# Attention, a gated MLP and a phase mixer in one launch: the pool of xT opened first, float64 by bit masks in wide pieces, 1/(2π) put into w_theta, and a new table for the order

## The chip, the cores and the metric

The kernel runs on one core of a Trainium2 chip. The metric is the device time of one execution in microseconds; executions of the kernel before took 879.43 us in the median of three, from 874.92 to 885.33 us. PE is TensorE, DVE is VectorE, ACT is ScalarE, POOL is GpSimd, and SP is SyncE, which here only issues transfers.

## The reference, cut to what matters

Batch 4, 8 heads, 576 positions, 64 columns a head, so 512 columns a position. The weights w_in, w_out, w_theta, w_tok and w_ch are float64 in memory, the rest is float32.

```python
scores = scale * q @ k.T + bias            # bias: a small network of log positions, one per head
x = softmax(scores) @ v                    # heads side by side: (4, 576, 512)

h = gelu_tanh(x @ w_in)                    # 512 -> 1024
u, v = h[..., :512], h[..., 512:]
v = w_sg @ layernorm(v) + b_sg             # 576 x 576 over the positions
x = x + (u * v) @ w_out

theta = x @ w_theta
y = w_tok_r @ (x * cos(theta)) + w_tok_i @ (x * sin(theta))
u = x + y
out = u + relu(u @ w_ch)
```

## The kernel before

**Tiles.** Heads go in pairs, so attention is 16 pairs (four batches by four), named by batch and pair: `xT0_2` belongs to batch 0, pair 2. A pair has nine score tiles of 128 rows by 576 columns: four for each head and one (kind 2) that holds the last 64 rows of both. A tile runs through every engine: scores `s` (PE, PSUM); `e`, the scores plus bias with their maximum (DVE, a custom operation); the exponential (ACT); `p`, a float16 upper part (ACT) and its residual (POOL, sometimes DVE); the transposed `pT` (a DMA transpose that SP issues); and `px`, the product with v (PE, one PSUM tile, 14 matmuls a score tile). After a pair's nine tiles the product is scaled into `xf` (four tiles) and `xfr` (the kind-2 tile), flipped by PE against the identity into `xq`, copied as two float16 parts into `xT` and also stored to memory. `xf` and `xfr` have one buffer each, `e` has four, `pT` eight.

**The MLP of a batch** reads `xT` and the converted `w_in` (`wi`): `vp`, gelu, the norm `n`, then `up` and `sp` (with w_sg), the product `gg` and its store. `s2` multiplies with w_out (`op`); `theta` makes `tp`, reduces it by multiples of 2π (`rk`, `rr`), takes sine and cosine and writes the products `z` in two parts; `ymix` (`yp`) mixes the positions, `s4` (`cp`) ends.

**PSUM.** The flips `xq`, the MLP's `vp`, `up` and `sp`, and the norms of the weights (`ps_wi`, `ps_ws`) share one ring of three buffers, handed out in the order in which the code asks for them (`cps`). A write to the ring therefore waits for the readers of the third request before it.

**SBUF.** Pools lie as a stack on each side. `xT` lives in pool `xTp`, opened after `w1_load` in `build`, so that it lies where the staging pool of `w1_load` (`wstage`, raw pieces of w_in and w_sg) was. A first write to it waits until that pool's work is done.

**Float64.** `conv64` turns a piece of raw pairs of words into float32. A weight's block of 128 rows goes in two halves of 256 (for w_tok 288) columns: three ACT operations (absolute value, sign, absolute value), two TENSOR_SCALAR and one SCALAR_TENSOR_TENSOR on DVE, and a product with the sign on POOL or DVE.

**The order.** The program is not run as written. A recorder (`Rec`) collects every operation with a key (its due time), an engine or a choice of engines, and what it depends on. `plan` lists the operations of each engine in the order of key plus `SHIFT[name]`, for a choice with `BIAS[name, engine]`, and emits them. All instructions are emitted by one helper line (379 before, 383 after), so the rows of the trace go by tile names. SP executes its list in order: loads and transposes stand in one queue, and an instruction whose buffer is not free holds those behind it.

**The stages of the profiled execution** (us from the start of the span): 0 to 108 the table of position biases (`hq` on DVE and ACT, `pb` on PE, `bs` on DVE or ACT); 108 to 238 pairs 0_1 to 0_3 with the conversion of w_in and w_sg; 238 to 441 batches 1 and 2 with the MLPs of 0 and 1; 441 to 539 batch 3 with MLP 2, and its drain; 539 to 690 MLP 3, `s2`, the conversion of w_out, w_theta, w_tok and w_ch, and the first `theta`; 690 to 880 the rest of `theta`, `ymix` and `s4`.

## Time and profile before

| | |
|---|---|
| median of three executions | 879.43 us (874.92 to 885.33) |
| the profiled execution | 881.56 us |
| its span, first to last instruction | 879.8 us |
| busy: PE | 762.3 us (87%) |
| busy: PE's weight loads, beside its matmuls | 534.8 us (61%) |
| busy: DVE | 629.9 us (72%) |
| busy: ACT | 520.5 us (59%) |
| busy: POOL | 298.4 us (34%) |
| moved by DMA | 115.52 MB, mean 131 GB/s |

The span is the time between the first and the last instruction of the profiled execution; about 1.8 us of its time lie around it. A busy share is a mean over stages with different limits, so the page's slices of 22 us and the sums by stage are read beside it.

### The profile page before, as it was taken

How to read it: one execution, taken by the hardware profiler on the slowest of the kernel's cores; microseconds unless marked ns; L12 is line 12 of the kernel's file. 1: busy time of each engine (PE TensorE's matmuls, PEld its weight loads, DVE VectorE, ACT ScalarE, POOL GpSimd, SP SyncE). 2: the span in 40 equal slices, each digit the busy share in tenths (PEclk: the TensorE clock that was granted, in tenths of full speed). 3: DMA queues.
4: the chain of work that ended last, by engine and by line, in shares of the span. 5: the costliest groups of instructions: out<-in, count | busy, mean ns of one | idle time of the engine just before them, and what ended most of it. 6: DMA issues, size and time to landing. Idle time of an engine off the chain costs nothing.

```text
span 879.8 us, 17586 instructions
## 1 busy us (share of the span) xinstructions
PE 762.3 (87%) x6544; PEld 534.8 (61%) x6544; DVE 629.9 (72%) x1475; ACT 520.5 (59%) x1038; POOL 298.4 (34%) x263
## 2 busy tenths in 40 slices
PE   5689778648899889997999976998878999999998
PEld 2234344326454555545654453687757999899998
DVE  5777558869698568986589754997989892763712
ACT  5777567865689447892579713655568671542500
POOL 0011244643567335672547531365433200000000
PEclk9979956557999999999799996999999999999999
DMA  7987689729898299866998396465622210010101
GB/s 227 217 169 172 169 184 192 150 87 192 158 186 154 72 221 179 169 150 133 190 188 151 77 179 159 133 198 173 180 82 64 74 54 1 1 55 1 41 14 54
DMA packets 205734, 115.52 MB, mean 131 GB/s; under 512 B 176593, under 2 KB 176849, under 8 KB 205649
## 3 DMA queue, kind: packets, MB, share of 16 engines
q1 hardware_dynamic: 198192, 101.01, 52.6%
q10 hardware_dynamic: 7456, 13.40, 5.0%
q8 instruction: 51, 0.84, 0.4%
q14 instruction: 35, 0.28, 0.1%
HBM read 47.13 MB, written 14.16 MB: 70 GB/s over the span
## 4 chain that ended last, share of the span: by engine, by line
PE 52%; DVE 17%; DMA 15%; issue 7%; ACT 5%; POOL 3%; SPq 1%; ACTq 0%; DVEq 0%; POOLq 0%
PE yp L379 12%; PE s L379 8%; PE cp L379 6%; DMA pT<-p 6%; PE pb L379 6%; PE sp L379 5%; PE tp L379 4%; PE up L379 4%; PE px L379 4%; PE vp L379 3%; POOL p L379 2%; DVE v L379 2%; DMA vr<-v_all 2%; DVE e L379 2%; DVE cvaw_tok L379 2%
## 5 line engine op out<-in xcount | busy, mean ns | idle before, releaser
L379 POOL TENSOR_TENSOR p<-e,p 128x576 f16<-128x576 f32 x144 | 191.0, 1338 | 183.3 <-ACT p L379 172.5
L379 PE MATMUL s<-kq 64*128 64x288 f32 (+1 forms) x640 | 149.1, 495 | 21.5 <-DVE m L379 21.5
L379 ACT ACTIVATE e<-e,m 128x576 f32<-128x576 f32 x144 | 110.6, 769 | 55.9 <-DVE m L379 44.7
L379 PEld LDWEIGHTS <-pT 128*128 128x128 f16 (+1 forms) x2240 | 86.0, 108 | 69.4 <-issue 30.4
L379 PE MATMUL px<-v,pT 128*128 128x64 f16 (+1 forms) x2240 | 95.4, 204 | 32.6 <-DMA pT<-p 21.9
L379 PE MATMUL yp<-wk,z 128*128 128x288 f32 x864 | 119.4, 297 | 1.5 <-ACT z L379 0.8
L379 DVE CUSTOM_DVE_ANT_0 e<-s,bias 128x576 f32<-128x576 f32 x128 | 94.6, 752 | 35.5 <-PE s L379 18.7
L379 PEld LDWEIGHTS yp<-wk,z 128*128 128x128 f32 x864 | 116.5, 190 | 2.6 <-ACT z L379 1.1
L379 PEld LDWEIGHTS s<-kq 64*128 64x128 f32 (+1 forms) x640 | 71.9, 199 | 65.8 <-DVE m L379 40.3
L379 ACT ACTIVATE p<-e 128x576 f16<-128x576 f32 x144 | 94.0, 674 | 29.7 <-DMA pT<-p 22.2
L379 PE MATMUL pb<-hq,w2s 128*32 128x288 f32 x576 | 69.3, 454 | 14.3 <-DVE bs L379 9.9
L379 PE MATMUL op<-sp_g,wo 128*128 128x288 f32 x384 | 60.8, 311 | 7.6 <-DVE x L379 4.1
L379 PE MATMUL vp<-wi,xT 128*128 128x512 f16 (+1 forms) x240 | 63.4, 397 | 1.4 <-DVE xT L379 1.4
L379 PEld LDWEIGHTS op<-sp_g,wo 128*128 128x128 f32 x384 | 54.4, 194 | 12.4 <-DVE x L379 4.9
L379 PEld LDWEIGHTS pb<-hq,w2s 128*32 128x32 f32 x576 | 28.4, 117 | 52.9 <-DVE bs L379 9.9
L379 PE MATMUL sp<-ws,n 128*128 128x64 f16 (+1 forms) x384 | 57.4, 287 | 0.3 <-DVE n L379 0.2
L379 PE MATMUL up<-xT,wi 128*128 128x64 f16 (+1 forms) x384 | 55.1, 287 | 0.7 <-DVE gtu L379 0.7
L379 ACT ACTIVATE sp_u<-x 128x576 fp32r<-128x576 f32 x16 | 10.8, 684 | 70.8 <-DVE x L379 70.1
L379 PE MATMUL cp<-sp_u,wc 128*128 128x288 f32 x384 | 52.5, 295 | 0.0
L379 PE MATMUL tp<-wt,sp_t 128*128 128x512 f32 x192 | 47.9, 403 | 4.3 <-DVE sp_t L379 2.6
L379 DVE TENSOR_SCALAR hq<-lt,sl,nb 128x576 f32<-128x576 f32 x96 | 49.8, 586 | 2.4 <-PE pb L379 1.6
L379 PEld LDWEIGHTS cp<-sp_u,wc 128*128 128x128 f32 x384 | 51.2, 188 | 0.2
(197 smaller groups left out, 1214.9 us busy)
## 6 DMA issues: line engine op xcount, KB each, us to landing
bias<-bs SPq DMA_DIRECT2D x32, 288.0 KB
kq<-kq SPq DMA_DIRECT2D x10, 576.0 KB
raww_tok<-w_tok SPq DMA_DIRECT2D x18, 288.0 KB
vr<-v_all SPq DMA_DIRECT2D x12, 384.0 KB
xx<-dx SPq DMA_DIRECT2D x16, 288.0 KB
out<-oo SPq DMA_DIRECT2D x16, 288.0 KB
dg<-gg SPq DMA_DIRECT2D x16, 256.0 KB
raw<-vp SPq DMA_DIRECT2D x12, 320.0 KB
```

What stands on the lines that cost most here:

```text
L379: getattr(getattr(self.nc, name), m)(*[res(x) for x in a], **out)
```

## The change

**Pools and buffers.** `xTp` is opened before `setup`, under all that is staged later, and is released last. `xf` has two buffers instead of one (`xfr` keeps one), `e` three instead of four, `pT` seven instead of eight. To make room, w_sg is loaded twice through one buffer (`ra`, then `rs`) instead of being kept, and v's sum of squares reads eight pieces of 1152 instead of twelve of 768.

**Float64.** With `fuse`, `conv64` takes a whole block (512 columns, for w_tok 576) at once: one ACT operation, two TENSOR_SCALAR and two SCALAR_TENSOR_TENSOR on DVE; the sign comes from a bit mask, and the product with it is gone. There are half as many loads, each twice as large. All five converted weights use it; the form with the sign stays in the code, unused.

**Theta.** w_theta is scaled by 1/(2π) when it is split, so that `tp` counts turns. A tile loses one TENSOR_SCALAR and one SCALAR_TENSOR_TENSOR of its DVE work; there are 18 tiles.

**Order.** The table is refitted, with an additional shift for each stage (`@a0` to `@a15` for the pairs, `@m`, `@o`, `@t`, `@y`, `@z` with the batch, `@w` and one for each weight). Against before, 36 residuals of `z` go from DVE to POOL, nine of the 36 `bs` additions go from DVE to ACT (18 and 18 before, 9 and 27 after), and the transfers of q and k go from ACT's queue to SP's (6 on ACT and 10 on SP before, 1 and 15 after). In bias_gen the matmuls of a group wait for all four `hq`.

```diff
-    def conv64(self, pool, dst, src, n, u):
+    def conv64(self, pool, dst, src, n, u, bufs, fuse=False):
...
-        nc.scalar.activation(a, hi.bitcast(F32), AF.Abs)
+        if fuse:
+            nc.scalar.activation(dst, hi.bitcast(F32), AF.Abs)
+            nc.vector.tensor_scalar(dst, dst, F64_MIN, F64_MAX, op0=ALU.max, op1=ALU.min)
+            nc.vector.tensor_scalar(di, di, 3, 0x3FFFFFF8, op0=ALU.logical_shift_left, op1=ALU.bitwise_and)
+            nc.vector.scalar_tensor_tensor(di, hi, TOP, di, op0=ALU.bitwise_and, op1=ALU.bitwise_or)
+            nc.vector.scalar_tensor_tensor(di, lo, 29, di, op0=ALU.logical_shift_right, op1=ALU.bitwise_or)
+            return
...
-        nc.vector.tensor_scalar(a, a, F64_MIN, F64_MAX, op0=ALU.max, op1=ALU.min)
-        nc.vector.tensor_scalar(ai, ai, 3, 0x40000000, op0=ALU.logical_shift_left, op1=ALU.bitwise_xor)
-        nc.vector.scalar_tensor_tensor(ai, lo, 29, ai, op0=ALU.logical_shift_right, op1=ALU.bitwise_or)
-        nc.scalar.activation(a, a, AF.Abs)
-        self.tt(("vector", "gpsimd"), dst, a, s, ALU.mult)
...
-        rs = sp.tile([P, 5, S], F32, name="rs")
...
+            rs = sp.tile([P, S], F32, tag="rs", bufs=1, name=f"ra{st}")
...
+            rs = sp.tile([P, S], F32, tag="rs", bufs=1, name=f"rs{st}")
...
-        s = a.tile([P, S], F32, tag="s", bufs=4, name=f"e{u}")
+        s = a.tile([P, S], F32, tag="s", bufs=3, name=f"e{u}")
...
-        pT = a.tile([P, 9, P], F16, tag="pT", bufs=8, name=f"pT{u}")
+        pT = a.tile([P, 9, P], F16, tag="pT", bufs=7, name=f"pT{u}")
...
-        xf = a.tile([P, 4, P], F32, tag="xf", bufs=1, name=f"xf{u}")
+        xf = a.tile([P, 4, P], F32, tag="xf", bufs=2, name=f"xf{u}")
...
-            nc.scalar.activation(k, ps, AF.Identity, scale=1.0 / (2 * math.pi), bias=self.magic)
-            nc.vector.tensor_scalar(k, k, MAGIC, None, op0=ALU.subtract)
-            nc.vector.scalar_tensor_tensor(r, k, -TWO_PI_HI, ps, op0=ALU.mult, op1=ALU.add)
-            nc.vector.scalar_tensor_tensor(r, k, -TWO_PI_LO, r, op0=ALU.mult, op1=ALU.add)
+            nc.scalar.activation(k, ps, AF.Identity, bias=self.magic)
+            nc.vector.scalar_tensor_tensor(r, k, MAGIC, ps, op0=ALU.subtract, op1=ALU.subtract)
...
+        self.p_x = nc.pool("xTp")
         self.setup()
...
         self.w1_load()
-        self.p_x = nc.pool("xTp")
...
-        for q in (self.ps_c, self.ps_x, self.p_c1, self.p_x, self.p_w1):
+        for q in (self.ps_c, self.ps_x, self.p_c1, self.p_w1, self.p_x):
```

Of the table, a line of each kind; the new `SHIFT` entries that begin with `@` are added to that of the name:

```diff
-    ("xT", "vector"): -9.533, ("xr", "scalar"): 42.3825, ("xr", "vector"): -78.4204,
+    ("xT", "vector"): -134.938, ("xr", "scalar"): -32.2441, ("xr", "vector"): 89.6171,
...
+    "@a0": -36.8725, "@a1": 84.4111, "@a10": -258.733, "@a11": -241.069, "@a12": 66.14, "@a13": 1.9727,
```

**Three places in the order.** First DVE where it first writes `xT`, in the second stage (108 to 238 us). `ih`, `gts`, `ghs` and `i2s` are small factors that follow the norm of one half of w_in, `v163` are pieces of v, `e0_3_1_3` is the score tile of pair 0_3, second head, last full tile. Before:

```order
L379 TENSOR_SCALAR gts0_132<-ih0_134 128x1
L379 TENSOR_SCALAR ghs0_133<-ih0_134 128x1
L379 CAST xT0_0_2097<-xq0_0_1802 128x512
L379 CAST xT0_0_2097<-xq0_0_2_2004 128x64
L379 TENSOR_TENSOR xT0_0_2097<-xq0_0_1802,xT0_0_2097 128x512
L379 ISA e0_3_1_3_2188,m0_3_1_3_1893<-s0_3_1_3_1925,bias3_75 128x576
```

Of the change:

```order
L383 TENSOR_TENSOR ih1_144<-fd_wi1_145,fd_v_152 128x1
L383 CAST xT0_0_170<-xq0_0_1509 128x512
L383 TENSOR_SCALAR i2s1_141<-ih1_144 128x1
L383 TENSOR_SCALAR ghs1_143<-ih1_144 128x1
L383 TENSOR_TENSOR xT0_0_170<-xq0_0_1509,xT0_0_170 128x512
L383 ISA e0_2_0_0_1494,m0_2_0_0_1429<-s0_2_0_0_1463,bias0_78 128x576
```

The first write of `xT0_0` has moved from the second half's factors (`ih0`) to the first half's (`ih1`), and from the eighth tile of pair 0_3 to the second tile of pair 0_2; the copy of the narrow flip `xq0_0_2`, which stood behind the first, is no longer beside it.

Second, DVE where the conversion of w_tok meets the first `theta`, at the end of the fifth stage (539 to 690 us). `tok4_0` is the first half of block 4, `wr_w_tok8` the whole block 8. Before:

```order
L379 TENSOR_SCALAR cvaw_tok4_0_8390<-cvaw_tok4_0_8390 128x288
L379 TENSOR_SCALAR rk0_4_8237<-rk0_4_8237 128x512
L379 TENSOR_SCALAR cvaw_tok4_0_8390<-cvaw_tok4_0_8390 128x288
L379 SCALAR_TENSOR_TENSOR rr0_4_8233<-rk0_4_8237,tp0_4_8145 128x512
L379 SCALAR_TENSOR_TENSOR cvaw_tok4_0_8390<-raww_tok4_0_8373,cvaw_tok4_0_8390 128x288
L379 SCALAR_TENSOR_TENSOR x1_3_8238<-xs3_0_8388,fd_v_153,op3_0_8336 128x576
L379 SCALAR_TENSOR_TENSOR rr0_4_8233<-rk0_4_8237,rr0_4_8233 128x512
L379 TENSOR_TENSOR wk_7223<-wr_w_tok3_8262,wk_7223 128x576
```

Of the change:

```order
L383 SCALAR_TENSOR_TENSOR wr_w_tok7_8031<-raww_tok7_8007,wr_w_tok7_8031 128x576
L383 SCALAR_TENSOR_TENSOR rr0_4_7982<-rk0_4_7986,tp0_4_7914 128x512
L383 SCALAR_TENSOR_TENSOR wr_w_tok7_8031<-raww_tok7_8007,wr_w_tok7_8031 128x576
L383 SCALAR_TENSOR_TENSOR x1_2_7096<-xs2_3_8081,fd_v_152,op2_3_8017 128x576
L383 TENSOR_TENSOR sp1_g3_8052<-gr3_1_7943,sp1_g3_8052 128x576
L383 TENSOR_TENSOR rw0_8045<-xp0_4_7912,rr0_4_7982 64x512
L383 TENSOR_SCALAR wr_w_tok8_8102<-wr_w_tok8_8102 128x576
L383 TENSOR_TENSOR wk_7097<-wr_w_tok7_8031,wk_7097 128x576
```

Theta's tile has one operation here where it had three, the conversion works on 576 columns, and it has come three to four blocks further by the same tile of theta.

Third, PE where MLP 2 ends and batch 3's attention drains, in the fourth stage (441 to 539 us). `sp2_3` and `sp2_4` are the last products of MLP 2, `s3_3_0_0` is the first score tile of the last pair's first head, and `xq3_0_2` the narrow flip of the batch's first pair. Before, where the last scores (of `s3_3_1_3`) stand 126 rows ahead of these:

```order
L379 LDWEIGHTS n16_2_5233
L379 MATMUL sp2_3_6694<-ws_1090,n16_2_5233 128x512
L379 LDWEIGHTS n16_2_5233
L379 MATMUL sp2_3_6694<-ws_1090,n16_2_5233 128x512
L379 MATMUL xq3_0_2_6697<-ident_160,xfr3_0_2_5526 128x64
```

Of the change:

```order
L383 MATMUL sp2_3_6457<-wsr_1078,nr_2_5064 128x512
L383 MATMUL s3_3_0_0_6482<-kq3_3_6127 128x288
L383 MATMUL s3_3_1_0_6504<-kq3_3_6127 128x288
L383 MATMUL s3_3_0_0_6482<-kq3_3_6127 128x288
L383 MATMUL s3_3_1_0_6504<-kq3_3_6127 128x288
L383 MATMUL xq3_0_2_6518<-ident_159,xfr3_0_2_5372 128x64
```

Scores of the last pair now stand between the last products of MLP 2; the last of them (`s3_3_1_3`) comes some 500 rows after these, among the products `px` of the last two pairs.

## Rows read from the trace of the kernel before

**Rows 1.** The page: busy tenths of PE, granted clock; 22 us a slice.

```profile
PE   5689778648899889997999976998878999999998
...
PEclk9979956557999999999799996999999999999999
```

**Rows 2.** Busy us by stage: stretch, length, each engine, clock, DMA share.

```profile
core 0: us, PE busy (x) PEld busy (x) DVE busy (x) ACT busy (x) POOL busy (x), PEclk, DMA share, GB/s
...
108.00:238.00 130.00, 91.91 (x774) 57.02 (x775) 97.38 (x293) 90.67 (x221) 62.30 (x56) 0.64 0.77 164
238.00:441.00 203.00, 186.60 (x1995) 109.31 (x1993) 153.37 (x416) 133.32 (x266) 111.84 (x93) 0.96 0.82 162
441.00:539.00 98.00, 81.04 (x917) 47.42 (x916) 69.18 (x186) 57.60 (x115) 47.98 (x41) 0.95 0.75 146
539.00:600.00 61.00, 60.54 (x369) 41.16 (x370) 52.46 (x110) 38.33 (x83) 25.00 (x23) 0.97 0.53 166
600.00:690.00 90.00, 74.95 (x497) 65.69 (x496) 83.20 (x149) 58.70 (x120) 35.98 (x31) 0.94 0.40 118
690.00:880.00 190.00, 185.58 (x1307) 178.88 (x1305) 101.53 (x164) 68.62 (x119) 5.27 (x6) 1.00 0.09 31
```

**Rows 3.** Tiles: ns min/median/max, first and last start; flip copies, norm.

```profile
L379 DVE CAST xT<-xq x32: 206/432/692, 205.4 to 538.4; 128x512 f16<-128x512 f32 x16, 128x64 f16<-128x64 f32 x16
...
L379 PE MATMUL ps_wi<-ssw,ones x4: 353/364/374, 164.1 to 196.0; 128*128 128x2 f32 x4
```

**Rows 4.** SP's queue, 167 to 215 us: start, us, issue, count.

```profile
167.51 1.32 SPq L379 DMA_TRANSPOSE pT<-p  x1
...
198.49 16.58 SPq L379 DMA_TRANSPOSE pT<-p  x8
```

**Rows 5.** Busy time in two short stretches, columns as in Rows 2.

```profile
160.00:200.00 40.00, 20.22 (x84) 11.89 (x85) 29.99 (x95) 30.61 (x81) 17.78 (x19) 0.50 0.44 106
520.00:536.00 16.00, 7.34 (x110) 4.94 (x109) 0.29 (x2) 0.68 (x1) 1.57 (x2) 0.80 0.97 162
```

**Rows 6.** DVE, ACT, POOL on cvawi, cvaw_tok, cvaw_theta, cvaw_ch, cvaw_out in turn.

```profile
0.00:880.00 880.00, 23.47 (x48) 12.93 (x32) 12.46 (x16) 0.92 0.58 131
...
0.00:880.00 880.00, 25.32 (x54) 15.69 (x36) 19.66 (x18) 0.92 0.58 131
...
0.00:880.00 880.00, 13.95 (x24) 6.78 (x16) 6.67 (x8) 0.92 0.58 131
...
0.00:880.00 880.00, 10.00 (x24) 6.50 (x16) 6.87 (x8) 0.92 0.58 131
...
0.00:880.00 880.00, 10.47 (x32) 6.64 (x16) 0.92 0.58 131
```

**Rows 7.** Tiles again: conversion of w_tok; theta's rk and rr.

```profile
L379 DVE TENSOR_SCALAR cvaw_tok<-cvaw_tok x36: 294/301/1348, 597.2 to 678.3; 128x288 f32<-128x288 f32 x18, 128x288 int32<-128x288 int32 x18
...
L379 DVE SCALAR_TENSOR_TENSOR cvaw_tok<-raww_tok,cvaw_tok x18: 444/448/946, 600.6 to 679.2; 128x288 int32<-128x288 int32 x18
...
L379 DVE TENSOR_SCALAR rk<-rk x18: 409/422/1516, 630.9 to 823.9; 128x512 f32<-128x512 f32 x18
...
L379 DVE SCALAR_TENSOR_TENSOR rr<-rk,rr x18: 677/684/1776, 634.8 to 826.4; 128x512 f32<-128x512 f32 x18
```

**Rows 8.** PE in time: a px group waits; then ACT's queue there.

```profile
532.50 0.93 PE L379 MATMUL px<-v,pT 128*128 128x64 f16 x14 [3.11 <-DMA pT<-p]
...
527.67 1.55 ACTq L379 DMA_DIRECT2D raww_out<-w_out  x2
```

**Rows 9.** A two-input operation on POOL, and z's residual on DVE.

```profile
L379 POOL TENSOR_TENSOR gg<-gg,gtu x20: 730/1277/1371, 283.4 to 611.6; 128x512 f32<-128x512 f32 x16, 128x256 f32<-128x256 f32 x4
...
L379 DVE TENSOR_TENSOR z<-rk,z x18: 677/684/1293, 645.6 to 832.2; 128x512 fp32r<-128x512 f32 x18
```

**Rows 10.** One score tile in time: e on DVE, its residual on POOL.

```profile
262.21 0.76 DVE L379 CUSTOM_DVE_ANT_0 e<-s,bias 128x576 f32<-128x576 f32 x1 [0.34 <-PE s L379]
...
266.68 2.52 POOL L379 TENSOR_TENSOR p<-e,p 128x576 f16<-128x576 f32 x2 [1.74 <-DVE mv L379]
```

More of the change, by code (lines that the diff above doesn't have):

```diff
@@ L253 @@
-    "xp": -331.5337, "xq": 298.6439, "xr": -67.349, "xs": -569.332, "xx": -233.673, "yp": -63.1746,
-    "z": 114.4221, "zb": 275.7247,
-}
-LOADF, LOADK = 1.8093412586188697, 8.575464505639914
-BV = 1.52008187476998
[5 rows of a table added]
+    "@w_ch": 85.8307, "@w_out": 57.1349, "@w_theta": 160.7065, "@w_tok": 95.8549, "@y0": -210.6919,
[3 rows of a table added]
+    "fa_ws": 1413.4328, "fb_v": 82.4448, "fb_wi": -819.9933, "fb_ws": -1094.933, "fc_v": 668.3878,
+    "fc_wi": -1320.5823, "fc_ws": 855.392, "fd_v": -186.6568, "fd_wi": -384.6853, "fd_ws": 954.7819,
@@ L729, in bias_gen @@
         self.ld(self.ident, d["ident"])
-        for i in range(12):
-            nc.key = 1.0 + 5 * i
-            vr = st.tile([P, 768], F32, tag="vr", bufs=2, name=f"vr{i}")
-            self.ld(vr, d["v_all"][:, i * 768:(i + 1) * 768], ("sync",))
+        for i in range(8):
+            nc.key = 1.0 + 7.5 * i
+            vr = st.tile([P, 1152], F32, tag="vr", bufs=2, name=f"vr{i}")
+            self.ld(vr, d["v_all"][:, i * 1152:(i + 1) * 1152], ("sync",))
             nc.scalar.activation(vr, vr, AF.Square, accum_out=self.ss_v[:, i:i + 1])
@@ L747, in w1_load @@
         self.eps4 = c.tile([P, 1], F32, name="eps4")
[L748 removed]
+        ssa = c.tile([P, 2, 4], F32, name="ssa")
         ssw = c.tile([P, 2, 2], F32, name="ssw")
@@ L1217, in build @@
         self.s2(0, t + 15, 3)
-        self.conv_w(self.wt, "w_theta", DM, 4, t + 15, 3)
+        self.conv_w(self.wt, "w_theta", DM, 4, t + 15, 3, 1.0 / TWO_PI)
         self.s2(1, t + 35, 3)
```

150 lines of the change are left out of this document (78 added, 72 removed), and 42 rows, old and new, of tables (BIAS, SHIFT).

## The prediction

> **What bounds the kernel now.** I read the page's slices first: PE is the busiest engine in most of them, and the granted clock stands near full except in slices 5 to 9 (counted from 0), 110 to 220 us, where it falls to 0.5 and PE's own digits are low [rows 1]. So I went by stage. The difference between a stage's length and PE's busy time is what the stage can give back without touching PE's work [rows 2]: 108 to 238 us, 130.0 − 91.9 = 38.1 us (at a clock of 0.64, so its matmuls run long as well); 238 to 441, 16.4; 441 to 539, 17.0; 539 to 690, 0.5 + 15.0 = 15.5; 690 to 880, 4.4. The last stage is PE's and gives nothing.
>
> Then the waits of each stage. In the second, the first copy of a flip into `xT` starts at 205.4 us and the last norm of w_in (`ps_wi`) is made at 196.0 [rows 3]; SP's queue issues no transpose between 167.5 + 1.3 and 198.5 us, and then eight in a row [rows 4]. The reader should see one chain in it: `xT0_0` cannot be written before the staging pool is done; its flips hold the PSUM ring and the only `xf`; the next pair's `xf`, then `px`, then the eight `pT` fill, and scores stop. From 160 to 200 us PE is busy 20.2 of 40 us at a clock of 0.50, its level of 1.2 GHz; 1.00, as in the last stage, is 2.4 GHz [rows 2, 5]. DVE is busy 97.4 of the 130 us, more than any other [rows 2]. From 520 to 536 us everything waits for transfers: DVE 0.3, PE 7.3 of 16 us, DMA share 0.97 [rows 5]. From 539 to 690 us DVE is busy 52.5 + 83.2 = 135.7 of 151 us beside PE's 135.5: two near-bounds, in turns [rows 2].
>
> **The change part by part.** The span is 879.8 us, of an execution of 881.56 us; the median is 879.43. These agree within 0.3%, so a sum made against the span is read as the time.
>
> *Second stage.* `xT` loses its wait for the staging pool, and w_in's conversion gets cheaper on DVE. Price of an operation on 512 columns: TENSOR_SCALAR 422 ns, SCALAR_TENSOR_TENSOR 684 ns (theta's `rk` and `rr`, medians) [rows 7]. A fused block of 512 takes 2 × 0.422 + 2 × 0.684 = 2.21 us, eight of them 17.7 us, where DVE spent 23.5 us [rows 6]: −5.8. POOL loses 12.5 us of products, and ACT's part shrinks from three operations a piece to one [rows 6]. DVE's work falls from 97.4 to about 91.6 us; at 80 to 90% of the time, where it is 75% now, the stage takes 102 to 115 us. The more cautious end, 114, gives **16** us. Bounds: 0 where the chain is only passed on (first rival); 25 if the stage reaches 92% busy with less work on DVE still (130 − 91.6/0.92 = 30, less 5 for PE's slower clock at the stage's start). The doubled loads of w_sg (5 × 576 columns) lie beside a DMA share of 0.77 [rows 2]; I cost them at nothing, since they are needed only when MLP 0 reaches `sp`, after the stage.
>
> *Third stage.* The two `xf` and the refitted order can take something of 16.4 us [rows 2]; fewer `e` and `pT` can cost. No row shows which. I take **5**, bounds 0 and 14: PE is already 92% busy.
>
> *Fourth stage.* Two loads of w_out are issued on ACT's queue at 527.67 us, among the last transposes [rows 8]; the group of `px` at 532.50 waits 3.1 us for `pT` [rows 8], with a similar wait after it. In the new order all w_out loads stand on SP behind the transposes: 5 us. Scores of the last pair move from the end of MLP 2, where PE is full, into this drain, where it is idle: 2 us more, of 16 − 7.3 = 8.7 idle in 520 to 536 [rows 5]. **7**, bounds 0 and 10.
>
> *Fifth stage.* Conversions of w_tok, w_theta, w_ch and w_out on DVE now take 25.3 + 14.0 + 10.0 + 10.5 = 59.8 us [rows 6]. For 576 columns I extend the lines from 288 to 512: TENSOR_SCALAR 301 to 422 gives 0.457, the other 448 to 684 gives 0.751 [rows 7]. Nine blocks at 2 × 0.457 + 2 × 0.751 = 2.42 make 21.7; twelve of 512 at 2.21 make 26.5; sum 48.3: −11.5. Undisturbed, two halves of a w_tok block cost 4 × 0.301 + 2 × 0.448 = 2.10 now, so for w_tok the gain is that its operations are no longer stretched (maximum 1348 ns against a median of 301 [rows 7]) while POOL multiplies. Theta's first batch, five tiles, loses 5 × (0.422 + 0.684) = 5.5 us; ten residuals of `z` at 0.684 go to POOL, 6.8 us [rows 7, 9]; some of w_ch is pulled forward into the stage, +5. DVE: −19 us. More than PE's idle time, 15.5, can't be won; I take **12**, bounds 0 and 15.5, since both engines' gaps don't close at once.
>
> *The residuals on POOL.* For a two-input operation on 512 columns POOL takes 1277 ns in `gg`, DVE 684 in `z` [rows 9]. In the last stage POOL is busy 5.3 of 190 us [rows 2], so the residuals, 26 of the 36, lie beside PE, unless `yp` waits for one. I take −**1**, bounds 0 and 36 × 0.593 = 21.3 (every one on the path). The Trainium skill, "GPSIMD Engine Reference", section "4.1 Engine selection", puts elementwise work on VectorE and says that GPSIMD takes about twice as long for two inputs. The trace agrees with 1277 against 684 ns; by that rule the move would cost up to the whole 21 us, by the row of POOL's idle time nearly nothing.
>
> *The rest.* Nine `bs` go from DVE to ACT in the first stage. No row here shows their duration; by the nearest two-input row, 0.68 us [rows 9], they are 6 us taken from one engine and given to the other, so between 6 us won and 6 us lost. I take 0, the middle, for v's pieces and the stricter wait of `pb` as well. q and k on SP: one issue a pair, each beside eight or nine transposes; 0.
>
> Sum: 16 + 5 + 7 + 12 − 1 = 39; 879.8 − 39 = 840.8, **841 us**.
>
> **The rivals.**
>
> *The flips stay held (17%).* `xq0_0_2` asks for the PSUM ring behind `ps_wi` of the second half, and `xfr` keeps one buffer. Then the second pair's end still waits for the last norm, made at 196 us [rows 3], and transposes pace the drain as before. Against it: the wide flip and `xf` go early in the new order. Only the fifth stage's 12, or with its bound 15.5 and 5 of the others, and less where POOL or fewer buffers cost: 13 to 29 us, 851 to 866.
>
> *Residuals on the path (8%).* If `yp` starts each of its tiles with the residual just made, POOL paces it: 841 + 21 = 862 us. For it: one residual follows another in all 18 tiles. Against it: the last stage has 190/26 = 7.3 us for each residual [rows 2], against 1.28 on POOL.
>
> *Three `e` buffers, slower (7%).* A tile's `e` is taken at 262.21 us and is free when POOL's residual has read it; POOL's row holds two tiles from 266.68 on, 1.26 us each, so the first is read by 267.94 [rows 10]: a life of 5.7 us. With three buffers a tile can't come oftener than every 5.7/3 = 1.9 us. Batches 1 and 2 have 72 tiles in the third stage's 203 us, 2.8 us a tile [rows 2]; evenly paced, the buffers decide once the life passes 3 × 2.8 = 8.4 us. At 10.7 us a tile takes 3.55: 72 × 0.73 = 53 us lost there, against the gain of 39, so 14 us slower, some 893 us. For it: tiles come in bursts, where the pace is quicker than the mean, and ACT and POOL get more work by the new order. Against it: that work (`bs`, `z`) lies in other stages, and the life now has 2.7 us of room.
>
> *More than forecast (10%).* DVE at 92% in the second stage (25), a smoother third (12), and the fifth to its bound (15.5), 7 and 5 from the fourth and the edges: 64 us, about 815.
>
> **How the numbers follow.** The forecast has 58%, its own range is 828 to 854. A measurement of this kernel can tell about 1% from no change, 870.6 us. Of the first rival's 17%, some 5% may reach no change if none of the fifth stage's gain shows; with the doubt between the second and the third rival, and of the forecast's tail, I give faster 0.85, same 0.08, slower 0.07. To hold eight of ten, the range takes the forecast's own, the first two rivals and a part of the fourth: 818 to 868.
>
> **What would show it.** Right: the first copy into `xT` well before 196 us, no gap of 30 us between transposes, a granted clock above 0.64 over 108 to 238 us and a shorter stage; DVE no longer above 90% from 600 to 690; `px` not waiting 3 us at the drain. Wrong: first copies early but `px` of the third pair still waiting at the old place (first rival); `yp` waiting for `z` from POOL (second); `e` on DVE waiting for POOL's `p` (third). The forecast falls if the second stage is not at least 8 us shorter.

## The result, and the profile after

The changed kernel takes 848.76 us in the median of four executions (847.74 to 857.60) against 879.94 of the kernel before in the same group: a ratio of 0.967 (95% interval 0.958 to 0.975). A second group of runs gave 852.83 against 881.33 us, 0.968 (0.962 to 0.973). The forecast was 841 us, in a range of 818 to 868, and faster. So the sign and the size were right; the sum was 39 us, and 31 came. Where they came from is another matter, and the profile shows it.

The page's busy tenths of PE and the granted clock of the changed kernel, in slices of 21 us, to be held against [rows 1]:

```profile
PE   4688698778999799997999879978699999999998
...
PEclk9899755589999999998999989999699999999999
```

The hollow of slices 5 to 9 in PE's row is shorter and shallower, but the clock still falls there, to 0.5 in slices 5 to 7.

Slices of equal length no longer mean the same work. So I cut both executions at landmarks: the last `pb` of the bias table, the first `vp` of MLP 0, the last `px` of the attention, the first `yp`, the end. Busy time between these landmarks, first of the kernel before and then of the changed one (columns as in [rows 2]):

```profile
0.00:101.00 101.00, 77.77 (x626) 32.94 (x626) 72.28 (x162) 68.11 (x105) 7.14 (x12) 0.93 0.79 187
101.00:218.40 117.40, 78.99 (x658) 49.42 (x656) 83.96 (x253) 84.08 (x207) 54.57 (x50) 0.61 0.77 165
218.40:536.20 317.80, 283.06 (x3089) 165.86 (x3088) 235.12 (x638) 201.38 (x405) 170.40 (x142) 0.96 0.80 158
536.20:662.20 126.00, 112.13 (x719) 85.15 (x717) 109.36 (x207) 75.71 (x158) 52.11 (x47) 0.95 0.50 152
662.20:879.80 217.60, 210.31 (x1461) 201.38 (x1459) 129.13 (x218) 91.23 (x165) 14.14 (x13) 0.99 0.11 36
```

```profile
0.00:86.40 86.40, 61.66 (x621) 24.73 (x624) 63.49 (x139) 70.68 (x105) 8.52 (x12) 0.96 0.83 214
86.40:189.60 103.20, 81.83 (x687) 51.59 (x680) 89.55 (x242) 71.79 (x149) 44.35 (x34) 0.62 0.96 206
189.60:497.60 308.00, 284.30 (x3069) 165.05 (x3068) 227.99 (x645) 207.32 (x408) 166.88 (x143) 0.97 0.83 163
497.60:628.80 131.20, 113.98 (x718) 88.08 (x715) 116.97 (x184) 59.48 (x97) 40.34 (x29) 0.90 0.54 169
628.80:845.90 217.10, 210.12 (x1463) 199.81 (x1461) 88.16 (x114) 73.65 (x124) 45.99 (x33) 1.00 0.06 23
```

| stretch | before | after | difference | terms of the forecast |
|---|---|---|---|---|
| to the last `pb` | 101.0 | 86.4 | −14.6 | 0 |
| to the first `vp` | 117.4 | 103.2 | −14.2 | −16 (second stage) |
| to the last `px` | 317.8 | 308.0 | −9.8 | −5 and −7 (third and fourth) |
| to the first `yp` | 126.0 | 131.2 | +5.2 | −12 (fifth) |
| to the end | 217.6 | 217.1 | −0.5 | +1 (`z` on POOL) |
| sum | 879.8 | 845.9 | −33.9 | −39 |

The middle three terms came nearly as worked out. The first stretch gave 14.6 us that I had put at nothing, and the fifth, in which the change removes the most instructions, got longer by 5.2. DVE's row there says why it is worth a closer look: 109.4 of 126.0 us busy before, 117.0 of 131.2 after. The work that was taken out of it has been replaced.

The second stretch is told by three rows. In the changed kernel the first copy into `xT` comes before the last norm of w_in, not after it as in [rows 3]:

```profile
L383 DVE CAST xT<-xq x32: 206/448/692, 128.0 to 499.8; 128x512 f16<-128x512 f32 x16, 128x64 f16<-128x64 f32 x16
```

```profile
L383 PE MATMUL ps_wi<-ssw,ones x4: 352/363/374, 125.1 to 158.2; 128*128 128x2 f32 x4
```

And SP, which stopped its transposes for 30 us in [rows 4], issues them here (start, us, issue, count):

```profile
124.48 13.57 SPq L383 DMA_TRANSPOSE pT<-p  x7
...
142.03 7.43 SPq L383 DMA_TRANSPOSE pT<-p  x3
...
150.18 4.15 SPq L383 DMA_TRANSPOSE pT<-p  x2
...
161.18 1.31 SPq L383 DMA_TRANSPOSE pT<-p  x1
```

The longest pause in this stretch is 161.18 − 150.18 − 4.15 = 6.9 us.

The drain of the last pair, where a group of `px` waited 3.11 us [rows 8]: its longest wait is now the 1.04 us of the first row below (PE in time), and the four loads of w_out are issued on SP, the first at 499.1 us, behind the last transpose (second row, of the tile's own view: minimum, median, maximum in ns, first and last start).

```profile
496.92 0.93 PE L383 MATMUL px<-v,pT 128*128 128x64 f16 x14 [1.04 <-DMA pT<-p]
```

```profile
L383 SPq DMA_DIRECT2D raww_out<-w_out x4: 333/335/382, 499.1 to 515.2; - x4
```

### The profile page after: what moved, and what is told of

Same layout as the page of the kernel before. It is cut to its first block, busy times and chain, and to the rows that moved or that the text cites. A ratio compares the mean times of both kernels' runs of the same rounds, so it can differ in the third digit from the quotient of the medians.

```text
span 845.9 us, 17245 instructions
## 1 busy us (share of the span) xinstructions
PE 751.9 (89%) x6544; PEld 529.3 (63%) x6544; DVE 586.2 (69%) x1323; ACT 482.9 (57%) x882; POOL 306.1 (36%) x250
## 4 chain that ended last, share of the span: by engine, by line
PE 51%; DVE 18%; DMA 12%; ACT 8%; issue 7%; POOL 4%; SPq 0%; ACTq 0%; POOLq 0%; DVEq 0%
PE yp L383 12%; PE s L383 9%; PE vp L383 6%; PE cp L383 6%; DMA pT<-p 5%; PE px L383 5%; PE up L383 4%; DVE e L383 3%; DMA bias<-bs 3%; PE tp L383 3%; POOL p L383 3%; PE sp L383 3%; DVE wr_w_tok L383 2%; ACT hq L383 2%; PE op L383 2%
## 5 line engine op out<-in xcount | busy, mean ns | idle before, releaser
L383 POOL TENSOR_TENSOR p<-e,p 128x576 f16<-128x576 f32 x144 | 191.7, 1341 | 191.4 <-ACT p L383 169.3
L383 PE MATMUL s<-kq 64*128 64x288 f32 (+1 forms) x640 | 152.9, 491 | 20.1 <-DVE m L383 19.0
L383 PEld LDWEIGHTS <-pT 128*128 128x128 f16 (+1 forms) x2240 | 86.8, 109 | 58.0 <-issue 33.2
L383 ACT ACTIVATE p<-e 128x576 f16<-128x576 f32 x144 | 94.9, 674 | 13.8 <-DMA pT<-p 12.3
L383 PE MATMUL op<-sp_g,wo 128*128 128x288 f32 x384 | 65.0, 324 | 15.2 <-DVE sp_g L383 7.9
L383 PEld LDWEIGHTS op<-sp_g,wo 128*128 128x128 f32 x384 | 58.2, 207 | 21.0 <-DVE sp_g L383 10.2
L383 PE MATMUL pb<-hq,w2s 128*32 128x288 f32 x576 | 54.6, 444 | 15.5 <-ACT bs L383 13.6
L383 DVE TENSOR_TENSOR x<-x,yp 128x576 f32<-128x576 f32 x16 | 12.1, 753 | 64.8 <-PE yp L383 64.8
L383 PEld LDWEIGHTS cp<-sp_u,wc 128*128 128x128 f32 x384 | 51.6, 188 | 0.2
L383 POOL TENSOR_TENSOR xs<-xx 128x576 f32<-128x576 f16 x16 | 25.0, 1560 | 73.9 <-DMA xx<-dx 43.7
L383 POOL TENSOR_TENSOR z<-rr,z 128x512 fp32r<-128x512 f32 x16 | 22.5, 1405 | 78.5 <-ACT z L383 73.1
```

The costliest lines, as they stand in the source:

```text
L383: getattr(getattr(self.nc, name), m)(*[res(x) for x in a], **out)
```

## The experiments

Each kernel is the changed one with one edit, unless the text says otherwise. The first expectations speak of the changed kernel as first profiled (span 845.9 us). It was run once more, together with three of the edits:

> The changed kernel once more, as the reference for the others of this group on the same chip: 846 to 858 us; from the last px to the end 348 us.

It took 852.83 us; its profiled execution has a span of 850.4 us. Two profiled executions of one program thus differ by 4.5 us, of which 1.3 lie before the last `px`, 2.0 between that and the first `yp`, and 1.2 behind. Six of the kernels below (w_ch late, z on DVE, conversion with sign, xs on DVE, the two together, theta as before) have the same order of PE's matmuls as the changed kernel up to the last `px`, and there it comes between 498.9 and 503.7 us. Differences of that size in one stretch of one profile say nothing; for these six I read the stretches behind the last `px`.

The landmarks of all profiled executions, in us (starts of the last `pb`, the first `vp`, the last `px`, the first `yp`; the span), with the medians and the ratios to the kernel before in the same group:

| kernel | last pb | first vp | last px | first yp | span | px to yp | median | ratio (95%) |
|---|---|---|---|---|---|---|---|---|
| before | 101.0 | 218.4 | 536.2 | 662.2 | 879.8 | 126.0 | 879.94 | 1 |
| after | 86.4 | 189.6 | 497.6 | 628.8 | 845.9 | 131.2 | 848.76 | 0.967 (0.958 to 0.975) |
| after, again | 86.8 | 190.6 | 498.9 | 632.1 | 850.4 | 133.2 | 852.83 | 0.968 (0.962 to 0.973) |
| xT on the staging pool | 86.2 | 210.8 | 510.6 | 651.3 | 869.2 | 140.7 | 871.95 | 0.989 (0.984 to 0.994) |
| pb two by two | 91.0 | 210.7 | 527.2 | 659.1 | 876.9 | 131.9 | 872.06 | 0.988 (0.981 to 0.994) |
| before, pb in groups | 93.3 | 207.5 | 532.9 | 667.3 | 885.0 | 134.4 | 886.60 | 1.006 (1.002 to 1.010) |
| pb not in groups | 82.6 | 198.1 | 511.7 | 653.2 | 871.6 | 141.5 | 873.37 | 0.991 (0.988 to 0.995) |
| w_ch late | 87.3 | 193.3 | 502.0 | 631.9 | 852.0 | 129.9 | 853.46 | 0.967 (0.963 to 0.972) |
| z on DVE | 85.4 | 191.2 | 500.7 | 636.6 | 851.4 | 135.9 | 853.67 | 0.968 (0.963 to 0.973) |
| conversion with sign | 87.3 | 191.3 | 498.9 | 633.5 | 850.7 | 134.6 | 854.90 | 0.970 (0.965 to 0.975) |
| xs on DVE | 87.6 | 191.8 | 503.0 | 632.8 | 850.7 | 129.8 | 851.31 | 0.966 (0.962 to 0.971) |
| w_ch late, xs on DVE | 85.2 | 191.4 | 501.7 | 626.9 | 844.3 | 125.2 | 844.82 | 0.957 (0.952 to 0.962) |
| theta as before | 86.4 | 192.2 | 503.7 | 642.0 | 863.9 | 138.3 | 866.05 | 0.983 (0.979 to 0.987) |
| one xf | 86.5 | 190.4 | 500.9 | 633.3 | 852.3 | 132.4 | 857.07 | 0.972 (0.969 to 0.976) |

One caution holds for the others: the order is planned anew for each kernel, and an edit in the first stages changes that of thousands of rows behind it, and their times with it.

### The place of xT

```diff
-        self.p_x = nc.pool("xTp")
         self.setup()
...
         self.w1_load()
+        self.p_x = nc.pool("xTp")
```

> The changed kernel with the pool of xT opened after w1_load again, as before the change; all else as changed. Theory of the prediction (its second stage): the stretch from the last pb to the first vp, 102.5 us in the changed kernel and 117.0 before, goes back by most of 14.5 us, the first copy into xT comes only after the last norm of w_in (158 us in the changed kernel), the total is 858 to 865 us. Rival (that stretch is shorter because the conversion is cheaper and the order is another): at most 4 us are lost, total 847 to 853.

Measured: 871.95 us, 19 to 23 above the changed kernel, and more than the expected 858 to 865. The first copy into `xT` comes at 193.6 us, 34 us behind the last norm of w_in, and `vp` starts at 210.8 (tile rows):

```profile
L383 DVE CAST xT<-xq x32: 201/452/693, 193.6 to 512.8; 128x512 f16<-128x512 f32 x16, 128x64 f16<-128x64 f32 x16
```

```profile
L383 PE MATMUL vp<-wi,xT x240: 379/379/635, 210.8 to 525.5; 128*128 128x512 f16 x96, 128*64 128x512 f16 x24
```

From the last `pb` to the first `vp` it is 124.6 us against 103.2 and 103.8: all of the second stretch's gain is gone, and more, while the stage before is as long as it was (86.2). So the changed kernel does not keep the second term without the new place of the pool. But it is not the old wait that came back. DVE in time around the first copy, first in this run, then in the kernel before:

```profile
169.92 2.73 DVE L383 SCALAR_TENSOR_TENSOR wi<-ri,fc_wi,wi 128x512 f16<-128x512 f32 x4
...
192.58 0.98 DVE L383 SCALAR_TENSOR_TENSOR wsr<-rs,fc_ws,wsr 128x576 f16<-128x576 f32 x1
193.60 0.82 DVE L383 CAST xT<-xq 128x512 f16<-128x512 f32 x2
```

```profile
199.29 2.73 DVE L379 SCALAR_TENSOR_TENSOR wi<-ri,fc_wi,wi 128x512 f16<-128x512 f32 x4
...
205.43 0.81 DVE L379 CAST xT<-xq 128x512 f16<-128x512 f32 x2
```

In this run w_in (`wi`) is done at 172.65 us, and the copy stands right behind the last piece of w_sg (`wsr`, done at 193.56), which the change loads a second time through one buffer of the same staging pool. In the kernel before w_in was the last, done at 202.02, and the last operation on w_sg started at 177.2. So a part of the 20 us is what the doubled loads of w_sg cost when `xT` lies where they are staged. And w_in is done some 30 us earlier than before with either place of the pool, which may have given a part of the −14.2 us by itself. How much of them is the pool's stays open: no run has the old place of the pool with w_sg kept as before.

What the place of the pool does is not quite what I had put down either. With `xT` late, the transposes of this run pause for at most 7.6 us (155.1 to 162.7), not for 30, I think because a second `xf` takes the next pair; what is late is MLP 0, which reads `xT`. By the last `px` 11.7 of the 20.2 us are left; another 7.5 come between `px` and `yp`, in a planned order that is another one there, and I don't put them down to the pool.

### One xf

```diff
-        xf = a.tile([P, 4, P], F32, tag="xf", bufs=2, name=f"xf{u}")
+        xf = a.tile([P, 4, P], F32, tag="xf", bufs=1, name=f"xf{u}")
```

> The changed kernel with one buffer of xf instead of two. By the prediction (two xf carry a part of the second and the third stage's gain): the waits of px for xf come back (5.2 us before, 2.0 in the changed kernel) and the total is 3 to 10 us longer, 856 to 863. Rival (with xT written early one xf is free in time): within 2 us, 851 to 855.

Measured: 857.07 us, 4.2 above the 852.83 of the changed kernel, with intervals of the ratio that overlap. The total lies in the range of the prediction's side (856 to 863), but its sign did not come: `px` waits 2.7 us for `xf`, against 2.0 in the changed kernel and 5.2 before, and the last `px` comes at 500.9 instead of 498.9, which is within the scatter. The second buffer is worth 4 us at most, once `xT` is written early. SP pauses for at most 7.2 us here (155.0 to 162.2). So the stall of [rows 4] is gone both with a late `xT` and two `xf` and with an early `xT` and one `xf`. This fits a stall that needed both causes; no run of the changed kernel has both of them back.

### The matmuls of the bias table

Three kernels on the first stretch. One exchanges the loops, so that two matmuls for the same 32 output partitions follow each other; it keeps the groups:

```diff
-            for n in range(2):
-                for q in range(4):
+            for q in range(4):
+                for n in range(2):
                     x = nc.tensor.matmul(
```

> The changed kernel with the two loops around the matmuls pb exchanged: the two halves of one hq follow each other, so that 144 of 288 matmuls write the same 32 output partitions as the one before them (62 in the kernel before, none in the changed one). The wait for all four hq stays. Theory (the first stage gained since matmuls for four different groups of partitions, one after the other, overlap on PE): PE's busy time on pb rises from 54.6 to above 69 us, the last pb ends at 100 us or later instead of 87.1, total 860 us or more. Rival (it gained by the bs additions moved from DVE to ACT and by the order of hq): pb stays at 52 to 58 us, the last pb ends by 91 us, total 846 to 853.

One is the kernel before with the groups alone:

```diff
-                    nc.tensor.matmul(ps[32 * q:32 * q + 32, n, :SH], w2f, hs[q][:, n * SH:(n + 1) * SH],
-                                     start=True, stop=True)
+                    x = nc.tensor.matmul(ps[32 * q:32 * q + 32, n, :SH], w2f, hs[q][0][:, n * SH:(n + 1) * SH],
+                                         start=True, stop=True)
+                    for _, o in hs:
+                        nc.dep(x, o)
```

> The kernel before with one part of the change: in the table of position biases the matmuls pb of a group wait for all four hq. Two of 288 matmuls then write the same 32 partitions as the one before them, instead of 62. Same theory: PE's busy time on pb falls from 69.3 to about 55 us, the last pb ends 8 to 14 us earlier than 101.4, total 865 to 873. Rival (the work moved from DVE to ACT made the gain): the last pb ends within 3 us of 101.4 and the total is 876 to 883.

And one is the changed kernel without them, its `bs` held to the engines that they have there:

```diff
-                    for _, o in hs:
-                        nc.dep(x, o)
...
+            nc.any(("vector", "tensor_scalar", (bv, ps[:, :, :SH], add, None), {"op0": ALU.add}) if G in
+                   (9, 12, 15, 18, 21, 24, 27, 30, 33) else
+                   ("scalar", "activation", (bv, ps[:, :, :SH], AF.Identity), {"bias": add}))
```

> The changed kernel with the matmuls pb of a group no longer held until all four hq are there, while the nine bs additions that DVE does in the changed kernel stay on DVE and the other 27 on ACT. Theory (grouping is what shortened the first stage, since four matmuls overlap when a group is complete): PE's busy time on pb rises from 54.6 to 60 us or more, the last pb ends 5 to 10 us later than 87.5, total 857 to 864. Rival (the division of bs between ACT and DVE and the order made the gain): the last pb ends within 2 us of 87.5.

The groups of `pb` on PE (busy us, mean ns of one, idle before and its releasers), in this order: before; after; exchanged loops; before with groups; after without groups:

```profile
L379 PE MATMUL pb<-hq,w2s 128*32 128x288 f32 x576 | 69.3, 454 | 14.3 <-DVE bs L379 9.9 <-ACT hq L379 2.2 <-DVE hq L379 1.6
```

```profile
L383 PE MATMUL pb<-hq,w2s 128*32 128x288 f32 x576 | 54.6, 444 | 15.5 <-ACT bs L383 13.6 <-DVE hq L383 1.1 <-DVE bs L383 0.2
```

```profile
L383 PE MATMUL pb<-hq,w2s 128*32 128x288 f32 x576 | 51.6, 480 | 23.9 <-ACT bs L383 22.8 <-DVE hq L383 1.1
```

```profile
L379 PE MATMUL pb<-hq,w2s 128*32 128x288 f32 x576 | 59.4, 473 | 18.4 <-DVE bs L379 12.6 <-DVE hq L379 3.2 <-ACT bs L379 2.0
```

```profile
L383 PE MATMUL pb<-hq,w2s 128*32 128x288 f32 x576 | 59.7, 443 | 9.9 <-ACT bs L383 7.0 <-DVE bs L383 1.5 <-DVE hq L383 1.3
```

All five do the same 576 matmuls of some 450 ns each; what differs is how many run at once. The four quarters of a group write different 32 partitions, and 576 × 0.444 = 256 us of matmuls in 54.6 us of busy time means that nearly five records overlap (the profile models the ends of matmuls, so this counts records, not work). In the kernel before it is 576 × 0.454/69.3 = 3.8: where the four `hq` come one by one, PE runs a group in parts. Exchanged loops do not disturb it (51.6 us), so the half of the first theory that spoke of neighbours on the same partitions is wrong. Groups in the kernel before take its `pb` from 69.3 to 59.4 us, and its last `pb` comes 7.7 us earlier, somewhat short of the expected 55 us and of the 8 to 14 us. Yet that kernel as a whole takes 886.60 us, where 865 to 873 were expected, and is slower than before: DVE starts the first score tile (`e`) at 64.9 us instead of 40.5, the last `px` is only 3.3 us earlier, and from `px` to `yp` it loses 8.4, in an order whose table was not fitted to it.

In the changed kernel the groups don't decide. Without them PE is busy on `pb` for 59.7 us instead of 54.6, but the last `pb` comes at 82.6, 4 us earlier. My theory falls there. That run loses its 20 us elsewhere: the last square of v comes at 95.4 us on ACT instead of 75.0, and with it the norm of v (`pbv`) at 97.0 instead of 87.1; 7.5 us are lost at the first `vp`, 12.8 at the last `px`, 21.1 at the first `yp`.

The run with exchanged loops is slow for another reason. Its plan put all 36 `bs` on ACT (27 in the changed kernel). ACT is busy 55.00 of 60 us from 30 to 90 us (the row below: start to end, length, busy), hardly more than the 54.46 of the changed kernel, but nine additions more are a part of it. Its last square of v comes at 106.4 instead of 74.7 us, and `pbv`, the norm that all of v waits for, at 108.6 instead of 86.8 (second row); the first `px` starts at 122.3 instead of 91.7.

```profile
30.00:90.00 60.00, 55.00 (x82) 0.89 0.74 171
```

```profile
L383 PE MATMUL pbv<-ssv,ones x2: 352/362/372, 108.6 to 108.8; 128*128 128x2 f32 x2
```

So from 60 to 90 us the first stretch was PE's in the kernel before (29.77 of 30 us busy); from 30 to 60 it was no engine's (the fullest, DVE, had 22.16, beside a DMA share of 1.01). In the changed kernel ACT is the fullest in both (27.01 and 27.45 of 30, PE 24.38 and 22.98). Of its 14.6 us the groups can explain up to 7.7, by the kernel before; the new order reaches the same without them. Which part of the new order it is, the division of `bs`, the sequence of `hq` or that of the loads, stays open.

### The last conversions held back

```diff
+            if u.startswith("w_ch"):
+                nc.dep(o, self.s2_last)       # o: the first operation of a block
```

> The changed kernel with the conversion of w_ch held until the last product of s2 is added (op's last reader), as an added dependence. Theory (in the fifth stage DVE is the bound, and the change pulled the conversion of w_ch, 10.8 us of DVE, and two blocks of w_tok forward into it from a stage in which DVE has room): the last op ends 4 to 9 us earlier than 617.3, and the total is 840 to 846. Rival (the stage is paced by other work, or w_ch only collides with theta there): the first yp comes within 2 us of 628.8 and the total is 847 to 853.

Measured: 853.46 us, the same as the changed kernel. The first `yp` comes 129.9 us after the last `px` (131.2 and 133.2), but the span from `px` to the end is 350.0 (348.3 and 351.5). The theory's 840 to 846 us did not come; the total is 0.5 us above the rival's range.

### The additions xs on DVE

```diff
-            nc.gpsimd.tensor_tensor(xs, xx[:, :S], xx[:, S:], op=ALU.add)
+            nc.vector.tensor_tensor(xs, xx[:, :S], xx[:, S:], op=ALU.add)
```

> The changed kernel with the 16 additions xs (two float16 parts of x) on DVE instead of POOL. In the fifth stage 8.5 to 12 us of DVE's busy time are operations that ran long while POOL worked on xs. Theory A (POOL's two-input operations lengthen DVE's, and that is the cost): DVE has 16 more operations of at most 0.75 us, 12 us, loses the 8.5 to 12 us of stretch, and op no longer waits for a late xs: from the last px to the end 340 to 348 us. Theory B (the long operations have another cause): the stretch stays, 12 us are added to a full engine, 354 to 361 us from the last px to the end.

Measured: 851.31 us; from `px` to the end 347.7 us against 351.5, at the upper end of theory A. First the reason for the theory, two operations of the changed kernel in time; POOL starts `xs` at 585.50, DVE two SCALAR_TENSOR_TENSOR at 585.80:

```profile
585.50 1.53 POOL L383 TENSOR_TENSOR xs<-xx 128x576 f32<-128x576 f16 x1 [2.97 <-DMA xx<-dx]
585.80 2.64 DVE L383 SCALAR_TENSOR_TENSOR wr_w_tok<-raww_tok,wr_w_tok 128x576 int32<-128x576 int32 x2
```

Undisturbed, the two take 2 × 0.75 = 1.50 us, and here 2.64: the first runs past the end of `xs` at 587.03 and then takes its usual time. The same group of operations over the whole run (minimum, median, maximum in ns), first of the changed kernel, then with `xs` on DVE:

```profile
L383 DVE TENSOR_SCALAR wr_w_tok<-wr_w_tok x18: 443/453/1545, 550.5 to 599.3; 128x576 f32<-128x576 f32 x9, 128x576 int32<-128x576 int32 x9
L383 DVE SCALAR_TENSOR_TENSOR wr_w_tok<-raww_tok,wr_w_tok x18: 743/751/1845, 553.5 to 603.0; 128x576 int32<-128x576 int32 x18
```

```profile
L383 DVE TENSOR_SCALAR wr_w_tok<-wr_w_tok x18: 441/448/460, 554.8 to 596.0; 128x576 f32<-128x576 f32 x9, 128x576 int32<-128x576 int32 x9
L383 DVE SCALAR_TENSOR_TENSOR wr_w_tok<-raww_tok,wr_w_tok x18: 744/748/1107, 557.0 to 599.4; 128x576 int32<-128x576 int32 x18
```

The medians stay, the maxima go from 1545 to 460 and from 1845 to 1107. All of DVE's work on `wr_w_tok` goes from 34.5 to 27.6 us. DVE does 16 additions more, of 750 ns each by their median, 12 us; from `px` to `yp` it is busy 118.0 us with them and 115.5 without, so 9.5 us of the 12 were there already, as stretch. `op` waits for `x` 0.2 us instead of 5.4, but for `sp_g` 10.7 instead of 7.9, and the first `yp` comes 3.4 us earlier. The cause is shown by the exchange: with POOL's `xs` gone, the long operations on `wr_w_tok` are gone but for one, of 1107 ns, which runs beside a `gg` on POOL. The Trainium skill has a rule for it, "SBUF — State Buffer", section "Who interferes with whom": of the pair of ports that VectorE and GpSimd share, whoever issues first has it for the whole instruction, and the other is blocked. The trace agrees, with 1845 ns for an operation of 751 that began 0.30 us behind an `xs`.

It matters who was first. In the changed kernel all nine operations on `wr_w_tok` that took over 100 ns more than their median began while an operation on POOL was running; five that began ahead of one kept their time. POOL's work is long in turn: its `xs` of 567.45 us, with three undisturbed operations of DVE beside it (one begun ahead of it, two behind its start), took 3.61 us, where the median is 1.40.

### Both together

```diff
+            if u.startswith("w_ch"):
+                nc.dep(o, self.s2_last)
...
-            nc.gpsimd.tensor_tensor(xs, xx[:, :S], xx[:, S:], op=ALU.add)
+            nc.vector.tensor_tensor(xs, xx[:, :S], xx[:, S:], op=ALU.add)
```

> The changed kernel with both edits that brought the first yp forward, each by about 3.4 us against a run of the changed kernel in the same kind of profile: w_ch's conversion held until the last product of s2 is added, and the additions xs on DVE. Theory (DVE's work ahead of the first yp is the bound of the fifth stage, and the two add up): the first yp 123 to 127 us after the last px (133.0 in the changed kernel), total 843 to 848. Rival (what is won before the first yp is lost behind it, since w_ch's conversion then meets theta): from the last px to the end 347 to 351 us, total 850 to 854.

Measured: 844.82 us, ratio 0.957 (0.952 to 0.962): 8.0 us under the changed kernel's 852.83, the fastest of all; its four executions (839.06 to 846.39) all lie below the eight of the changed kernel (847.74 to 857.60). Time and first `yp` are as the theory expected. The last two stretches of it, as above:

```profile
501.70:626.90 125.20, 111.14 (x714) 87.09 (x712) 112.39 (x191) 57.36 (x92) 16.17 (x14) 0.92 0.55 172
626.90:844.30 217.40, 212.21 (x1467) 201.09 (x1466) 91.17 (x123) 76.49 (x129) 46.08 (x33) 1.00 0.07 25
```

From `px` to `yp` it takes 125.2 us, where the two profiles of the changed kernel take 131.2 and 133.2, and nothing is given back in the last stretch (217.4). DVE is busy 112.4 us there instead of 117.0. Each edit alone moved the median by at most 1.5 us; only together do they shorten the whole. So DVE's work ahead of the first `yp` does bound the fifth stretch.

### The conversion with the sign

```diff
-            self.conv64(self.p_st, r[:, :ncol], self.d[name][:, i], ncol, f"{name}{i}", 2, True)
+            self.conv64(self.p_st, r[:, :ncol], self.d[name][:, i], ncol, f"{name}{i}", 2, False)
```

> The changed kernel with w_out, w_theta, w_tok and w_ch converted in wide pieces, but with the sign as before the change: three operations on ACT, two TENSOR_SCALAR and one SCALAR_TENSOR_TENSOR on DVE, and the product with the sign on DVE or POOL. Theory A (the bit masks give the fifth stage time, but other edits take it away): from the last px to the end 355 us or more instead of 348, total 855 to 865. Theory B (the masks only exchange one operation for another of the same length, so they give nothing there): 346 to 351 us from the last px to the end, total 847 to 853.

Measured: 854.90 us, 2.1 above the changed kernel with overlapping intervals; from `px` to the end 351.8 against 351.5. That is theory B's account, though the measured numbers lie 0.8 and 1.9 us above its ranges: the bit masks themselves give nothing that can be measured. On DVE they exchange a product for a second SCALAR_TENSOR_TENSOR, 34.5 us on `wr_w_tok` with them and 35.3 without. They save ACT two of three operations, and ACT has room there (59.4 of 133.2 us busy).

### Theta, and the residuals of z

```diff
+            nc.vector.tensor_scalar(k, k, MAGIC, None, op0=ALU.subtract)
-            nc.vector.scalar_tensor_tensor(r, k, MAGIC, ps, op0=ALU.subtract, op1=ALU.subtract)
+            nc.vector.scalar_tensor_tensor(r, k, -6.28125, ps, op0=ALU.mult, op1=ALU.add)
+            nc.vector.scalar_tensor_tensor(r, k, 6.28125 - TWO_PI, r, op0=ALU.mult, op1=ALU.add)
```

> The changed kernel with theta as before: w_theta not scaled, and one TENSOR_SCALAR and one SCALAR_TENSOR_TENSOR more on DVE for each of 18 tiles. By the prediction (five of these tiles lie in the fifth stage, 5.5 us of DVE): total 4 to 8 us above the changed kernel's 852.8, 856 to 861. Rival (theta's operations are a chain of one tile and the tiles overlap, and the last stage is PE's): within 2 us, 851 to 855.

Measured: 866.05 us, 13.2 above the changed kernel, above the ranges of both sides and more than the forecast's term had. From `px` to `yp` it is 5.1 us, as the prediction priced theta's first batch; from `yp` to the end 221.9 instead of 218.3, 3.6 us in a stretch that I had called PE's alone; the rest of the profile's difference, 4.8, lies ahead of the last `px`, where the order is the same. Scatter in one profile can be that large (503.0 there in the run with `xs` on DVE, of 851.31 us in all), but all four executions of this kernel lie above 862, so what makes up these 4.8 us stays open.

```diff
-    ("z", "gpsimd"): 39.2968, ("z", "vector"): 80.4866,
+    ("z", "gpsimd"): 639.2968, ("z", "vector"): -80.4866,
```

> The changed kernel with the 36 residuals of z back on DVE by the choice of engine in the table. By the prediction (residuals on POOL cost 1 us, up to 21.3 if all were on the path): the same within 4 us, 847 to 853. Rival A (POOL's residuals hold yp, or stretch DVE's operations, 10 us of stretch in the last stage): 835 to 843. Rival B (DVE's ten residuals before and around the first yp are missed): 4 to 7 us slower, 853 to 857.

Measured: 853.67 us, the same. In the last stretch POOL is idle, DVE is busy 95.1 instead of 88.2 us, and it takes 214.8 us instead of 218.3 (the row below, to be held against the changed kernel's last row above); before the first `yp` the run loses 2.7.

```profile
636.60:851.40 214.80, 209.96 (x1460) 200.19 (x1460) 95.12 (x143) 71.47 (x121) 0.00 (x0) 1.00 0.06 23
```

Neither rival A's 10 us nor the 21.3 us of the prediction's rival are there as time. The stretch that rival A spoke of is there as busy time: over the whole run DVE does 36 operations more, 24.7 us by their median of 685 ns, and is busy only 12.7 us more (597.3 against 584.6). It costs nothing, since PE is busy 97 to 98% of the last stretch with either engine.

## Why the prediction was right, and where it was not

**The second stage** (−16, came −14.2) came in its size, and its mechanism is shown in part. The stall is gone: the first copy into `xT` is written 30 us ahead of the last norm, and the transposes' 6.9 us exclude that the flips stay held (first rival). The way to the 16 us was wrong in one step. It let DVE's work fall by 5.8 us, since w_in's conversion was to take 17.7 us instead of 23.5 [rows 6]. It took 14.9 + 8.9 us (busy us, mean ns in the rows below; 14.2 + 7.3 in the second profile), as operations of it ran long beside POOL's (up to 1497 ns for one input and 1761 for two):

```profile
L383 DVE SCALAR_TENSOR_TENSOR ri<-rawwi,ri 128x512 int32<-128x512 int32 x16 | 14.9, 948 | 0.0
L383 DVE TENSOR_SCALAR ri<-ri 128x512 f32<-128x512 f32 (+1 forms) x16 | 8.9, 576 | 0.1
```

Between the landmarks DVE's busy time even rose, from 84.0 to 89.6 us (88.1 in the second profile), and PE's, 79.0 before, was 81.8 and 75.3; what fell is idle time, from 33.4 to 13.7 us on DVE and from 38.4 to 21.4 on PE (15.7 and 28.5 in the second). The mechanism also had one link too many: with two `xf` the transposes no longer depend on `xT`, and what then waits is MLP 0. And how much the pool gave and how much the earlier w_in stays open, as said above. One of the signs that I gave is not clear: the granted clock between the landmarks is 0.62 and 0.67 in the two profiles, where it was 0.61.

**The third and fourth stages** (−5 and −7, came −9.8 together) were right in sum. At the drain the longest wait of `px` fell from 3.11 to 1.04 us, and all of its waits for `pT` there from 8.7 us (526 to 537) to 2.8 (488 to 498.5), so 5.9 of the 7 us are seen as waits. No run undoes the loads of w_out, the place of the last scores, or the numbers of `e` and `pT`; their parts are argued from these rows.

**The fifth stage** (−12, came +5.2) is the step that failed, in its size and in its sign. I had priced the removed and the added operations, and the prices of the added ones were exact in the median: 453 and 751 ns by the row above, against 457 and 751 worked out. Three things were wrong. First, "−11.5" compared undisturbed new operations with disturbed old ones, and took for granted that the stretching would go with POOL's products. It stayed, since POOL's `xs` and `gg` go on. DVE's conversion of w_tok took 18.0 + 11.0 = 29.0 us by the rows of its two operations (without the residuals `wk`), against the 21.7 that I had worked out and 25.3 before [rows 6]; with `xs` off POOL it is 13.8 + 8.1 = 21.9. All four conversions of the stage took 61.6 us by the rows of their operations, where I had worked out 48.3 and it was 59.8: the −11.5 came as +1.8. Second, "+5" for conversions pulled forward was too low: all 36 wide operations of w_tok and 13 of 16 of w_ch now run ahead of the first `yp`, where before it was 44 of 54 narrow ones of w_tok and none of w_ch; w_ch with two of its residuals alone is 10.8 us. Third, they stand on DVE together with the splits `sp_g` and the additions `x` that `op` waits for. PE's waits after the last `px`, first of the changed kernel and then of before (waiting for, us in total, times, longest):

```profile
PE op L383 <- DVE sp_g L383: 7.9, 6, 2.3
PE op L383 <- DVE x L383: 5.4, 4, 3.7
```

```profile
PE op L379 <- DVE x L379: 4.1, 5, 1.7
...
PE op L379 <- DVE sp_g L379: 1.1, 1, 1.1
```

Together with its waits for splits on ACT, `op` waits 15.2 us, where it was 7.6 before, and 10.3 in the run with both edits. My sign for this stage came nevertheless: in the 90 us around the first `yp` that were 600 to 690 before, DVE is busy 74.9 us instead of 83.2, but what it has to do ahead of them is more. The 6.8 us of `z`'s residuals are not seen either: with them back on DVE it is 350.7 us from the last `px` to the end, against 351.5. The run with both edits shows that DVE's order and POOL's sums are this stage's limit: 6 to 8 us came back by moving work, without removing any.

**The first stage** (0, came −14.6) was missed. I had looked at which engine does the `bs` additions and at nothing else; the profile said that PE was busy 29.77 of 30 us there from 60 to 90 while its matmuls, at 454 ns and 576 of them, could overlap further. With a price of 0 ± 6, from a row of another operation, this term had no reading of the stage behind it. That the total came so near the forecast is luck: two errors of 14.6 and −17.2 us nearly cancel.

**The rivals.** The 13 to 29 us of the first rival do not follow from its own terms, which give 12, or 15.5 + 5 = 20.5. Residuals on POOL as a cost: not there. Three `e` buffers: DVE's `e` waited 14.5 us for POOL in all of the kernel before and 19.6 in the changed one, 5 us, far from 53; the forecast's −9.8 came in spite of it. Theta's term was too small in the sum: 5.5 us were put down for the stage ahead of `yp` and 5.1 came, but 3.6 more came behind it.

## What to carry to other kernels

A gain on an engine is a gain in time only if the room it leaves is not filled from behind: list what the new order pulls forward into the stage, with its price, before the removed work is summed. Compare like with like, a disturbed mean with a disturbed mean, and ask of each stretched operation which engine's work stretched it and whether the change takes that away. And a stage that looks untouched by a change is still read for its bound; here the one priced at nothing gave as much as the stage with the largest term.
